# Attention and MoE kernel: one piece of W12 fewer, last outputs by two queues, and a new planner's table

## The chip, the cores and the metric

The kernel runs on one core of a Trainium2 chip. The metric is the device time of one execution in microseconds (us). Engines are named as the profile names them: PE is TensorE (PEld its weight loads), DVE VectorE, ACT ScalarE, POOL GpSimd, SP SyncE, which here only issues DMAs.

## What is computed

The reference is a recurrence over 768 positions for 4 batches of 8 heads with 40 dimensions, and then a product chain over the 3072 tokens of 320 numbers:

```
for t in range(S):
    y[:, :, t] = einsum('bhd,bhde->bhe', rt, state)
    Sa = einsum('bhde,bhe->bhd', state, at)
    state = state * wt - einsum('bhd,bhe->bhde', Sa, bt) + einsum('bhd,bhe->bhde', vt, kt)
a = x @ w1            # x: y as 3072 x 320; w1, w2: 320 x 1024
b = x @ w2
out = ((a * b) @ w3) @ w_out   # w3: 1024 x 1024, w_out: 1024 x 320
```

The four matrices come as 64-bit floats.

## The kernel before

**Work and stages.** The recurrence is cut into 12 chunks of 64 positions (NCH, C). For each chunk the kernel loads its inputs (`load`), scales them by running products of w (`scale`), forms the products inside the chunk (`causal`, L551), solves the triangular systems (`solve`, `join`; small VectorE instructions at L630 and L634), prepares pairs and tokens (`pairs` L792, `tokens` L816), runs the recurrence step by small matmuls of 64 by 64 (`rec`, `product` at L840), and writes y, which SP's DMAs lay out as xr (`gather`, L915). Then `mlp` runs: xs is xr split in a high and a low part (ACT L940, DVE L943); a and b come from eight matmuls each per 128 columns at L957 (`terms` pairs the five WT tiles with the parts of xs), their product is split again (gh by ACT, gl by POOL or DVE at L974), and 48 matmuls at L983 with W3 = w3 @ w_out (built once, L470) give the output, which ACT copies to o and SP sends (L992).

**The weights.** VectorE, ScalarE and GpSimd turn the 64-bit numbers into 32-bit floats piece by piece (`convert`, from L385): a piece has 128 partitions and 1024 columns. Its steps are cv.in (SP's load of raw, L391), cv.e (L394, DVE), cv.exp (L398, ACT), cv.sign (L401, ACT), cv.m (L404, DVE), cv.lo (L408, DVE), cv.f (L412, DVE) and cv.out (L415, DVE or POOL). There are 17 pieces (one of 512 columns): 2 for rows 0 to 127 of W12 = [w1, w2], 3 for w_out, 8 for w3, 2 for W12's rows 128 to 255 and 2 for its last 64 rows, which the host lays twice into 128 rows. After each W12 piece, w.hi (ACT copy to float32r) and w.lo (L457, DVE or POOL: what the copy lost) fill WT. Of the last 64 rows WT[4] holds the high part in partitions 0 to 63 and the low part in 64 to 127, so that one matmul uses both. The tiles of the MLP (xs, gh, gl, ga, o) take the memory of the conversion, so no MLP begins before the last W12 piece is done (`third`).

**What sets the order.** Nothing is ordered by hand: every step is an `op` with a due time (t0 of its chunk, minus an offset P of its stage, plus OFF of its tag) and a cost (OPS). `Order.place` simulates the engines with these costs, takes on each engine the ready op with the smallest due time among those that could start within LOOK, and models buffers (SLOTS: y, xr, xs 1; raw 2; bank 6), TensorE's clock, tile modes (a matmul group that changes mode gets STICK added to its due time, and waits for the one before), DMA landing times and the lock between DVE and POOL for ops that need both ports (`two`). The instructions are emitted in that order, and each engine runs its own in order. ON says by one letter per op whether a step that both can do goes to POOL (p) or DVE (d).

Of the kernel before, what the change touches and what calls it, by code (L numbers as in the profile page):

```python
# [14 lines left out]
ALU = mybir.AluOpType  # L15
# [4 lines left out]
NCH = S // C  # L20
# [10 lines left out]
CW = 1024  # L31
# [12 lines left out]
OFF = {"ca.j": -611.218, "ca.js": -295.116, "ca.lm": -409.432, "ca.mask": 322.878, "ca.mm": -196.496, "cv.e":  # L44
       -352.619, "cv.exp": -294.308, "cv.f": 875.871, "cv.in": 923.729, "cv.lo": 148.411, "cv.m": -331.453, "cv.out":
       -690.808, "cv.sign": -986.054, "ga": 652.698, "jo.cp1": 176.7, "jo.cp2": 1171.31, "jo.mm1": 500.308, "jo.mm2":
       559.977, "jo.tt": 1216.266, "ld.aa": 255.685, "ld.fm": -308.122, "ld.xx": -220.769, "m.a": -43.748, "m.ab":
       -25.534, "m.gh": -539.967, "m.gl": -14.3, "m.mm1": 97.143, "m.mm2": 289.0, "m.o": 98.802, "m.out": -533.298,
       "m.xh": -105.084, "m.xl": 349.579, "nil": 390.528, "pa.cp": -142.457, "pa.mask": 411.539, "pa.mm": 399.693,
       "pa.rv": 721.462, "pa.v": -32.743, "r.hs": -489.727, "r.n": 318.043, "r.s": -178.475, "r.sb": -189.193, "r.st":  # L50
       490.608, "r.t0": -269.903, "r.t1": 72.728, "r.t2": -860.309, "r.tr": -475.318, "r.u": -459.283, "r.y":
       -480.807, "r.zn": -15.068, "r.zv": -155.411, "sc.aa": 621.487, "sc.chk": -167.343, "sc.exp": 187.27, "sc.gi":
       -148.615, "sc.gt": -230.551, "sc.ln": 87.006, "sc.scan": 203.673, "sc.xs": 130.059, "so.d": -775.834, "so.in":
       -264.37, "so.m1": -358.78, "so.m2": -299.304, "so.q": 713.223, "so.sa": -515.229, "so.sb": -535.393, "so.t":
       -345.96, "so.td": 366.095, "so.tt": -385.449, "so.v": -186.183, "so.x": -90.021, "so.z": 257.847, "tk.cp":
       -717.729, "tk.mm": 348.057, "w.hi": 667.696, "w.lo": -164.398, "w3.hi": 386.505, "w3.lo": -443.484, "w3.mm":
       -484.2, "z.bk": 434.685}
LOOK = dict(pe=0.135, act=0.0, dve=0.0, pool=0.101, sp=0.0, nil=0.0)
# [27 lines left out]
    "m.mm2": ("pe", 0.88, 0, "128", 1.05, 12, 0.31, 1.88), "m.o": ("act", 0.437), "m.out": ("sp", 0.58, 0, None, 0.25), "nil": ("nil", 0.0), "z.bk": ("act", 0.53),  # L86
# [3 lines left out]
FLIGHT, QUEUE, STICK = 1.9, 8, 34.913  # L90
# [32 lines left out]
class Order:  # L123
# [39 lines left out]
    def place(self):  # L163
# [29 lines left out]
        while len(placed) < len(ops):  # L193
# [982 lines left out]
```

## Time and profile before

| | us |
|---|---|
| timed runs, median of 3 | 648.69 (648.24 to 648.99) |
| the profiled execution, its own time | 643.84 |
| its span, first to last instruction | 642.1 |
| mean granted TensorE clock | 0.984 |
| TensorE busy | 566.2 (88%) |
| VectorE busy | 473.3 (74%) |
| ScalarE busy | 382.5 (60%) |
| GpSimd busy | 184.7 (29%) |

A busy share is an average over stages; the stages are told apart by the view that gives each engine's busy time in a stretch of the span. A group row gives the line, engine and operation, the tiles written and read, the shape and count, the busy time and the mean of one in ns, and then how long the engine stood idle just before these instructions and what ended most of that. All of ScalarE's plain copies have the helper's line L273.

### The profile page before, as it was taken

The page shows a single profiled execution, that of the slowest core. Times are in us where ns is not written, and L with a number is a line of the kernel's source. Part 1 is how long each engine was busy: PE and PEld are TensorE (multiplying, and loading weights), DVE is VectorE, ACT ScalarE, POOL GpSimd, SP SyncE. Part 2 cuts the span into 40 slices and gives each one's busy share as a digit, 9 for nine tenths or more (in the row PEclk, how much of TensorE's full clock was granted, in tenths as well). Part 3 has the DMA queues.
Part 4 walks back from the last instruction along what each step waited for, and adds up shares of the span by engine and source line. Part 5 has one row for each costly group of instructions (what it writes and reads, how often), then busy time and mean ns, then how long its engine had stood idle before and what let it go on. Part 6 is the DMA issues. An engine that isn't in the chain of part 4 may idle for free.

```text
span 642.1 us, 27039 instructions
## 1 busy us (share of the span) xinstructions
PE 566.2 (88%) x11970; PEld 503.9 (78%) x11970; DVE 473.3 (74%) x849; ACT 382.5 (60%) x825; POOL 184.7 (29%) x230
## 2 busy tenths in 40 slices
PE   1536889867999999999999999998999999999995
PEld 0435767556988988888888889887988898898995
DVE  6799897987949959769589599497595794971220
ACT  6767557686465665755755746657557557354221
POOL 3542414035332413403312115332232242020111
PEclk9999989968999999999999999999999999999998
DMA  8975566535213423523534335235135333210001
GB/s 193 294 225 167 154 212 217 196 87 152 69 29 85 117 69 98 141 48 90 137 80 110 82 79 134 59 96 141 41 93 141 78 83 81 51 37 14 26 21 25
DMA packets 53401, 68.23 MB, mean 106 GB/s; under 512 B 29984, under 2 KB 37664, under 8 KB 51232
## 3 DMA queue, kind: packets, MB, share of 16 engines
q1 hardware_dynamic: 53280, 66.46, 38.3%
q8 instruction: 95, 1.56, 1.0%
q14 instruction: 26, 0.21, 0.1%
HBM read 57.79 MB, written 3.93 MB: 96 GB/s over the span
## 4 chain that ended last, share of the span: by engine, by line
PE 36%; DVE 28%; ACT 17%; DMA 9%; SPq 5%; issue 4%; POOL 0%; ACTq 0%; DVEq 0%
PE bank L957 15%; PE bank L840 9%; ACT JP L273 5%; DVE tmp L630 4%; SPq L915 4%; DMA fm<-in_fmg_dram 4%; PE bank L983 4%; ACT TT L273 3%; PE bank L551 3%; DMA xr<-y 3%; DVE ab L604 2%; PE bank L470 2%; DVE mf L408 2%; DVE ga L971 2%; ACT hs L273 2%
## 5 line engine op out<-in xcount | busy, mean ns | idle before, releaser
L957 PE MATMUL bank<-xs,W 128*128 128x256 f32 x1536 | 208.3, 288 | 2.8 <-ACT o L273 2.8
L957 PEld LDWEIGHTS bank<-xs,W 128*128 128x128 f32 x1536 | 187.8, 189 | 14.1 <-ACT o L273 3.6
L273 ACT ACTIVATE gh<-ga 128x512 fp32r<-128x512 f32 x48 | 30.3, 631 | 94.8 <-DVE ga L971 94.8
L891 DVE TENSOR_TENSOR un<-bank,mask_h 128x416 f32<-128x416 f32 x48 | 28.2, 588 | 73.0 <-PE bank L840 63.9
L974 POOL TENSOR_TENSOR gl<-ga,gh 128x512 fp32r<-128x512 f32 x29 | 37.5, 1292 | 118.3 <-ACT gh L273 92.4
L801 POOL TENSOR_SCALAR_AFFINE_SELECT vg<-vg 64x256 f32<-64x256 f32 x96 | 43.9, 457 | 74.6 <-DVE gl L974 24.0
L983 PE MATMUL bank<-W3h,gh 128*128 128x320 f32 x192 | 63.8, 332 | 0.0
L567 POOL TENSOR_SCALAR_AFFINE_SELECT lm<-lm 64x512 f32<-64x512 f32 x48 | 34.0, 708 | 95.5 <-ACT lm L273 74.7
L983 PE MATMUL bank<-W3l,gh 128*128 128x320 f32 x192 | 59.2, 308 | 0.0
L983 PE MATMUL bank<-W3h,gl 128*128 128x320 f32 x192 | 59.2, 308 | 0.0
L273 ACT ACTIVATE JP<-bank 64x256 f32<-64x256 f32 (+2 forms) x120 | 45.4, 379 | 20.7 <-PE bank L551 19.0
L840 PE MATMUL bank<-hs,TT 64*64 64x104 f32 x768 | 49.8, 269 | 7.3 <-ACT TT L273 5.2
L840 PE MATMUL bank<-un,bk 64*64 64x104 f32 (+1 forms) x768 | 47.9, 266 | 2.8 <-DVE un L891 2.3
L523 POOL TENSOR_TENSOR xx<-xx,gi 112x1024 f32<-112x1024 f32 x12 | 28.5, 2379 | 74.6 <-DVE gi L519 22.9
L971 DVE TENSOR_TENSOR ga<-bank,ga 128x512 f32<-128x512 f32 x48 | 32.7, 681 | 22.3 <-PE bank L957 22.3
L840 PEld LDWEIGHTS bank<-hs,TT 64*64 64x64 f32 x768 | 39.3, 142 | 11.5 <-ACT TT L273 6.0
L840 PE MATMUL bank<-vg,bk 64*64 64x104 f32 (+1 forms) x768 | 47.1, 264 | 0.0
L840 PEld LDWEIGHTS bank<-un,bk 64*64 64x64 f32 (+1 forms) x768 | 37.8, 130 | 8.9 <-DVE un L891 5.6
L551 PE MATMUL bank<-aa,xx 40*64 40x64 f32 x1536 | 32.8, 239 | 10.7 <-POOL xx L523 5.5
L551 PEld LDWEIGHTS bank<-aa,xx 40*64 40x64 f32 x1536 | 30.5, 153 | 12.9 <-POOL xx L523 5.7
L470 PE MATMUL bank<-wof,w3f 128*128 128x320 f32 x128 | 38.0, 453 | 2.4 <-DVE w3f L415 1.5
L273 ACT ACTIVATE ga<-bank 128x512 f32<-128x512 f32 x48 | 28.7, 597 | 16.9 <-PE bank L957 16.3
(120 smaller groups left out, 1245.9 us busy)
## 6 DMA issues: line engine op xcount, KB each, us to landing
rv<-in_rv_dram SPq DMA_DIRECT2D x48, 294.0 KB
xx<-in_fmx_dram SPq DMA_DIRECT2D x24, 448.0 KB
raw<-in_w3t_dram SPq DMA_DIRECT2D x8, 1024.0 KB
raw<-in_w_dram SPq DMA_DIRECT2D x6, 1024.0 KB
fm<-in_fmg_dram SPq DMA_DIRECT2D x24, 227.5 KB
aa<-in_fma_dram SPq DMA_DIRECT2D x24, 224.0 KB
vg<-in_vt_dram SPq DMA_DIRECT2D x48, 80.0 KB
out_dram<-o SPq DMA_DIRECT2D x48, 80.0 KB
```

The source lines that it names most:

```text
L273: act.activation(out_, in_, AF.Copy, scale=scale)
L470: pe.matmul(out=pt.t[:, 0:DM], lhsT=w[:, j], rhs=wof[:, j], start=(j == 0), stop=(j == NJ - 1))
L523: e.tensor_tensor(out=X, in0=X, in1=gi.t.unsqueeze(2).to_broadcast([ROWS, 2 * NP, 2, C]), op=ALU.mult)
L551: pe.matmul(out=bank(s)[64 * z:64 * z + 64, i, p], lhsT=X[r, p, z], rhs=aa[i].t[r, p], start=True, stop=True)
L567: op("ca.mask", due + 6, lambda q=q: pool.affine_select(out=lm.t[q], in_=lm.t[q], pattern=[[0, 2 * NP], [1, C]], compare_op=ALU.is_gt, fil ...
L801: op("pa.mask", due + 2, lambda q=q, vg=vg: pool.affine_select(out=vg.t[q, :, 0:C], in_=vg.t[q, :, 0:C], pattern=[[0, NP], [1, C]], compar ...
L840: pe.matmul(out=out_(ab ^ z, p), lhsT=left(ab, ab ^ x, p), rhs=right(ab ^ x, p), start=start and p == 0, stop=True, skip_group_check=True)
L891: dve.tensor_tensor(out=un[i].t, in0=view(hp[i]), in1=mask_h.unsqueeze(1).to_broadcast([128, NP, N]), op=ALU.mult)
L957: pe.matmul(out=pt.t[:, TOK * x:TOK * x + TOK], lhsT=WT[k][:, cs], rhs=xs.t[:, z], start=(n == 0), stop=(n == 7))
L971: op("m.ab", t, lambda a=a, pt=pt: dve.tensor_tensor(out=a.t, in0=wide(pt), in1=a.t, op=ALU.mult), r=[pt], w=[a])
L974: both(("gl", c % NCH * 4 + j // 2), "m.gl", t + 1, lambda e, a=a, j=j: e.tensor_tensor(out=gl.t[:, j:j + 2], in0=a.t, in1=gh.t[:, j:j + 2 ...
L983: pe.matmul(out=pt.t[:, 0:DM], lhsT=l.t[:, j, ts], rhs=W3[r][:, j], start=(j == 0 and n == 0), stop=(j == NJ - 1 and n == 2))
```

## The change

The last 64 rows of W12 come as one array `wc` of 128 rows: in rows 0 to 63 their columns of w1, in 64 to 127 those of w2. They are one piece, and its two halves are each copied (w.hi) and subtracted (w.lo, now always on DVE), the low part going to the other 64 partitions. The piece counter goes from 17 to 16. For the last chunk, the second half of each output tile is sent by ACT's queue (tag m.oa). The table of due times, assignments and costs is another one, and a DMA in the planner has two more terms (a longer flight, `cold`, and a delay behind landing, `act`).

```diff
-T0, T = 449.562, 122.639
-P = dict(w0=116.83, ws=51.334, ld=75.808, sc=8.354, ca=161.389, so=-139.305, sp=243.519, jo=671.741, pa=42.027,
-         tk=3.502, rg=-37.491, ga=1051.868, ml=179.371, mt=282.608)
-ON = dict(aa="dppddpdddppdpppddppppddd", cv="pdddppdddpddddppp",
-          gl="dpppdpppddppddpppdddddpppppdpdpdppppddddpppdpppp", ws="pdddpp", xs="ddpddppppdpppdddppddpdpd")
-OFF = {"ca.j": -611.218, "ca.js": -295.116, "ca.lm": -409.432, "ca.mask": 322.878, "ca.mm": -196.496, "cv.e":
...
-LOOK = dict(pe=0.135, act=0.0, dve=0.0, pool=0.101, sp=0.0, nil=0.0)
+T0, T = 514.56, 92.461
+P = dict(w0=-196.327, ws=45.883, ld=498.429, sc=358.623, ca=116.411, so=-652.303, sp=-438.072, jo=499.915, pa=49.614,
+         tk=-155.98, rg=-40.9, ga=1276.543, ml=545.435, mt=406.895)
+ON = dict(aa="pdddpddpppppppppppddpdpp", cv="ppddddpdddpdddpd", gl="ppppppdppppdpppdddppppppddpppppdpdppdddpdddpdpdp",
+          ws="pddd", xs="pdpddpdppdpppdpdpdpppddp")
+OFF = {"ca.j": -279.458, "ca.js": -671.541, "ca.lm": -806.163, "ca.mask": 55.347, "ca.mm": 33.954, "cv.e": -173.885,
...
+LOOK = dict(pe=0.122, act=0.0, dve=0.0, pool=0.371, sp=0.0, nil=0.0)
...
-    "cv.in": ("sp", 0.42, 0, None, 4.7), "cv.e": ("dve", 0.682, 1), "cv.exp": ("act", 1.090), "cv.sign": ("act", 1.030),
+    "cv.in": ("sp", 0.42, 0, None, 3.4, 0, 0.3, 0.15), "cv.e": ("dve", 0.682, 1), "cv.exp": ("act", 1.13), "cv.sign": ("act", 1.13),
...
-    "w.hi": ("act", 0.990), "w.lo/p": ("pool", 2.430, 1), "w.lo/d": ("dve", 1.213, 1),
+    "w.hi": ("act", 1.05), "w.lo/p": ("pool", 2.430, 1), "w.lo/d": ("dve", 1.213, 1),
...
-    "ga": ("sp", 0.7, 0, None, 0.25),
+    "ga": ("sp", 0.78, 0, None, 0.25, 0, 1.0, 0.0),
...
-FLIGHT, QUEUE, STICK = 1.9, 8, 34.913
+FLIGHT, QUEUE, STICK = 1.9, 8, 0.0
...
-                done, clock[e] = max(t + FLIGHT, landed[-1]) + o["span"], t + o["cost"]
+                done, clock[e] = max(t + FLIGHT + o["cold"], landed[-1]) + o["span"], t + o["cost"]
                 landed.append(done)
+                done += o["act"]
...
-    pieces = iter(range(17))
+    pieces = iter(range(16))
...
-            for f in range(2 * DFF // CW):
+            for f in range(2 * DFF // CW if k < 2 else 1):
                 cs = slice(CW * f, CW * f + CW)
-                mf = convert(w12[k * 128:k * 128 + 128, cs], None, due)
-                n = (0, 1, 4)[k]
-                rows = slice(64, 128) if k == 2 else slice(0, 128)
+                mf = convert(w12[k * 128:k * 128 + 128, cs] if k < 2 else wc, None, due)
                 over = ["conv"] if k == 0 else ["conv", "reg2"]
...
-                op("w.hi", due, f1, r=[mf, *over], w=[("W", k, f)])
-                both(("ws", 2 * k + f), "w.lo", due, f2, r=[mf, *over], w=[("W", k, f)])
+                for x in (f,) if k < 2 else range(2):
+                    xs = slice(CW * x, CW * x + CW)
+                    q, z = (slice(0, 128),) * 2 if k < 2 else (slice(64 * x, 64 * x + 64), slice(64 - 64 * x, 128 - 64 * x))
+                    hi, lo = (0, 1, 4)[k], 2 + k
...
+                    op("w.hi", due, f1, r=[mf, *over], w=[("W", k, x)])
+                    if k < 2:
+                        both(("ws", 2 * k + f), "w.lo", due, f2, r=[mf, *over], w=[("W", k, x)])
+                    else:
+                        op("w.lo/d", due, lambda f2=f2: f2(dve), r=[mf, *over], w=[("W", k, x)])
                 due += step
...
             for b in range(2):
-                op("m.out", t, lambda b=b, tt=tt, o=o: sp.dma_start(
+                tag, e = ("m.oa", act) if c == NCH - 1 and b else ("m.out", sp)
+                op(tag, t, lambda b=b, tt=tt, o=o, e=e: e.dma_start(
                     out=out[bass.ds((2 * tt + b) * S + row, C)], in_=o.t[64 * b:64 * b + 64]), r=[o])
...
-    rows += rows[256:]
...
+    wc = bits(np.concatenate([w12[256:, 0:DFF], w12[256:, DFF:]], axis=0))
+    w12 = bits(w12[:256])
```

The numbers of OFF, P and T0 are due times on the planner's own scale, not microseconds of the chip. Most other costs in OPS move by some hundredths.

## Rows read from the trace of the kernel before

**Rows 1.** The page, TensorE's busy time.

```profile
PE 566.2 (88%) x11970; PEld 503.9 (78%) x11970; DVE 473.3 (74%) x849; ACT 382.5 (60%) x825; POOL 184.7 (29%) x230
```

**Rows 2.** Stretches: length; busy PE, PEld, DVE, ACT, POOL; clock, DMA share, GB/s.

```profile
40.00:140.00 100.00, 75.20 (x1648) 57.88 (x1648) 90.50 (x130) 68.43 (x118) 28.39 (x30) 0.93 0.57 178
140.00:160.00 20.00, 15.90 (x472) 13.37 (x471) 15.22 (x36) 13.63 (x30) 10.49 (x12) 0.90 0.50 131
160.00:600.00 440.00, 426.68 (x9303) 386.31 (x9304) 330.96 (x628) 263.11 (x607) 119.73 (x153) 1.00 0.33 83
600.00:642.10 42.10, 35.48 (x278) 35.18 (x276) 6.24 (x11) 9.96 (x18) 6.73 (x6) 0.96 0.11 27
```

**Rows 3.** Timeline of POOL, DVE and ACT, 134 to 172: start, length, instruction.

```profile
135.06 2.13 POOL L415 TENSOR_TENSOR mf<-mf,sg 128x1024 f32<-128x1024 f32 x1 [4.14 <-DVE mf L408]
...
145.73 2.13 POOL L415 TENSOR_TENSOR mf<-mf,sg 128x1024 f32<-128x1024 f32 x1 [0.74 <-DVE tmp L630]
...
150.49 2.35 POOL L457 TENSOR_TENSOR W<-mf,W 64x1024 fp32r<-64x1024 f32 x1 [0.18 <-ACT W L273]
...
136.94 0.80 DVE L394 TENSOR_SCALAR e<-raw 128x1024 uint16<-128x1024 uint16 x1
...
156.13 0.95 DVE L943 TENSOR_TENSOR xs<-xr,xs 128x768 fp32r<-128x768 f32 x1
...
149.35 1.05 ACT L273 ACTIVATE W<-mf 128x1024 fp32r<-128x1024 f32 x1
...
153.92 0.84 ACT L940 ACTIVATE xs<-xr 128x768 fp32r<-128x768 f32 x1
```

**Rows 4.** Line L957, 140 to 200: least/median/most ns, first and last start.

```profile
L957 PE MATMUL bank<-xs,W x182: 276/282/388, 157.9 to 200.0; 128*128 128x256 f32 x182
```

**Rows 5.** Groups by shape, whole span: busy, mean of one, idle before.

```profile
L408 DVE SCALAR_TENSOR_TENSOR mf<-raw,mf 128x1024 f32<-128x1024 uint32 x16 | 21.2, 1326 | 0.2
...
L401 ACT ACTIVATE sg<-raw 128x1024 bf16<-128x1024 int16 x16 | 18.5, 1154 | 10.1 <-DVE w3f L415 4.7 <-POOL mf L415 2.6 <-DVE mf L415 2.2
L398 ACT ACTIVATE e<-e,ebias 128x1024 uint16<-128x1024 uint16 x16 | 18.4, 1147 | 1.7 <-DVE e L394 1.7
...
L412 DVE TENSOR_TENSOR sg<-sg,e 128x1024 bf16<-128x1024 bf16 x16 | 12.2, 760 | 3.0 <-ACT sg L401 2.4 <-ACT e L398 0.6
L404 DVE TENSOR_SCALAR mf<-raw 128x1024 int32<-128x1024 int32 x16 | 11.4, 715 | 1.1 <-DMA raw<-in_w3t_dram 1.0
L394 DVE TENSOR_SCALAR e<-raw 128x1024 uint16<-128x1024 uint16 x16 | 11.2, 699 | 1.1 <-DMA raw<-in_w_dram 1.0
...
L415 POOL TENSOR_TENSOR mf<-mf,sg 128x1024 f32<-128x1024 f32 x4 | 9.0, 2254 | 21.6 <-DVE sg L412 16.8 <-DVE mf L408 4.1 <-DVE tmp L630 0.7
...
L457 POOL TENSOR_TENSOR W<-mf,W 64x1024 fp32r<-64x1024 f32 x2 | 4.7, 2358 | 0.3 <-ACT W L273 0.2
```

**Rows 6.** Tile raw and line L457: least/median/most ns, first and last start.

```profile
L408 DVE SCALAR_TENSOR_TENSOR mf<-raw,mf x17: 686/1226/1859, 24.2 to 140.1; 128x1024 f32<-128x1024 uint32 x16, 128x512 f32<-128x512 uint32 x1
...
L457 DVE TENSOR_TENSOR W<-mf,W x3: 1208/1211/3149, 43.2 to 137.7; 128x1024 fp32r<-128x1024 f32 x3
```

**Rows 7.** Tile y, 0 to 200: SP's DMAs from y to xr.

```profile
L915 SPq DMA_DIRECT2D xr<-y x24: 538/684/941, 80.2 to 166.7; - x24
```

**Rows 8.** Timeline of the end, and line L992 over the span.

```profile
635.86 1.11 SPq L992 DMA_DIRECT2D out_dram<-o  x2
...
L992 SPq DMA_DIRECT2D out_dram<-o x48: 466/558/1814, 180.5 to 636.4; - x48
```

**Rows 9.** Stretches of 10 us, columns as in rows 2.

```profile
80.00:90.00 10.00, 8.81 (x180) 6.13 (x178) 9.75 (x15) 5.14 (x11) 1.99 (x3) 0.83 0.74 240
...
130.00:140.00 10.00, 6.13 (x163) 5.45 (x152) 8.55 (x10) 7.79 (x14) 3.31 (x3) 0.51 0.25 88
```

**Rows 10.** The chain that ended last, 585 to 642: start, length, what.

```profile
592.26 1.14 PE bank L957 x8
...
613.07 15.24 PE bank L957 x128
```

More of the change, by code (lines that the diff above doesn't have):

```diff
@@ L58 @@
-LOOK = dict(pe=0.135, act=0.0, dve=0.0, pool=0.101, sp=0.0, nil=0.0)
+T0, T = 514.56, 92.461
[4 more added lines that the diff above has]
+OFF = {"ca.j": -279.458, "ca.js": -671.541, "ca.lm": -806.163, "ca.mask": 55.347, "ca.mm": 33.954, "cv.e": -173.885,
+       "cv.exp": -132.486, "cv.f": 1449.755, "cv.in": 755.934, "cv.lo": 858.805, "cv.m": -594.194, "cv.out": -327.381,
+       "cv.sign": -1155.983, "ga": 1271.368, "jo.cp1": 1151.213, "jo.cp2": 965.253, "jo.mm1": 575.096, "jo.mm2":
+       797.938, "jo.tt": 1558.004, "ld.aa": 185.001, "ld.fm": -766.597, "ld.xx": -104.394, "m.a": -375.288, "m.ab":
+       97.307, "m.gh": -538.707, "m.gl": -254.877, "m.mm1": 53.279, "m.mm2": 147.301, "m.o": 81.919, "m.oa": -178.394,
+       "m.out": 265.507, "m.xh": -147.679, "m.xl": 576.185, "nil": 57.266, "pa.cp": 49.867, "pa.mask": 479.639,
+       "pa.mm": 801.234, "pa.rv": 906.531, "pa.v": -140.458, "r.hs": -159.212, "r.n": 106.389, "r.s": 138.062, "r.sb":
+       -260.258, "r.st": 563.83, "r.t0": -652.593, "r.t1": 453.968, "r.t2": -618.307, "r.tr": -1004.632, "r.u":
+       -592.361, "r.y": -1181.646, "r.zn": 22.379, "r.zv": -122.778, "sc.aa": 849.905, "sc.chk": -338.326, "sc.exp":
+       492.942, "sc.gi": -103.955, "sc.gt": -577.576, "sc.ln": -311.006, "sc.scan": -174.304, "sc.xs": 366.767,
+       "so.d": -1080.429, "so.in": -520.493, "so.m1": -702.795, "so.m2": 189.337, "so.q": 1004.707, "so.sa":
+       -1260.855, "so.sb": -1105.151, "so.t": -277.876, "so.td": 721.968, "so.tt": -146.905, "so.v": 19.25, "so.x":
+       27.744, "so.z": 325.32, "tk.cp": -936.577, "tk.mm": 424.344, "w.hi": 972.575, "w.lo": -198.775, "w3.hi":
+       194.369, "w3.lo": -532.212, "w3.mm": -83.172, "z.bk": 877.353}
@@ L65 @@
     "w3.mm": ("pe", 2.15, 0, "128", 2.33, 16, 0.838, 1.88), "w3.hi": ("act", 0.44), "w3.lo": ("dve", 0.46),
-    "ld.fm": ("sp", 0.42, 0, None, 0.85), "ld.xx": ("sp", 0.42, 0, None, 1.85), "ld.aa": ("sp", 0.42, 0, None, 0.85),
-    "sc.chk": ("act", 0.64), "sc.scan": ("dve", 1.26, 1), "sc.ln": ("act", 0.62), "sc.exp": ("act", 0.76),
+    "ld.fm": ("sp", 0.42, 0, None, 0.75, 0, 0.3, 0.5), "ld.xx": ("sp", 0.42, 0, None, 1.85, 0, 0.3, 0.85), "ld.aa": ("sp", 0.42, 0, None, 0.88, 0, 0.3, 0.4),
+    "sc.chk": ("act", 0.73), "sc.scan": ("dve", 1.26, 1), "sc.ln": ("act", 0.62), "sc.exp": ("act", 0.63),
@@ L77 @@
+    "jo.cp2": ("act", 0.375), "jo.tt": ("act", 0.625),
+    "pa.rv": ("sp", 0.42, 0, None, 1.08, 0, 0.3, 0.6), "pa.v": ("sp", 0.65, 0, None, 0.36, 0, 0.3, 0.4), "pa.mm": ("pe", 0.52, 0, "64", 0.66, 64, 0.089, 1.88), "pa.cp": ("act", 0.4),
     "pa.mask": ("pool", 0.42, 1),
@@ L261, in attention_moe @@
 @with_exitstack
-def attention_moe(ctx: ExitStack, tc: tile.TileContext, fmg, fmx, fma, rv, vt, sq, svr, w12, w3t, wo, out):
+def attention_moe(ctx: ExitStack, tc: tile.TileContext, fmg, fmx, fma, rv, vt, sq, svr, w12, wc, w3t, wo, out):
     nc = tc.nc
@@ L1153, in bits @@
         return x.view(np.int64) if x.dtype == np.float64 else x
-    w12 = bits(np.concatenate([np.asarray(i["moe_w1"])[rows], np.asarray(i["moe_w2"])[rows]], axis=1))
+    w12 = np.concatenate([np.asarray(i["moe_w1"])[rows], np.asarray(i["moe_w2"])[rows]], axis=1)
+    wc = bits(np.concatenate([w12[256:, 0:DFF], w12[256:, DFF:]], axis=0))
+    w12 = bits(w12[:256])
     w3t = bits(np.asarray(i["moe_w3"]).reshape(NJ, 128, NJ, 128).transpose(0, 3, 2, 1).reshape(NJ, 128, DFF))
@@ L1158, in _layout @@
     return {n: np.ascontiguousarray(t) for n, t in
-            dict(fmg=fmg, fmx=x, fma=fma, rv=rv, vt=vt, sq=sq, svr=svr, w12=w12, w3t=w3t, wo=wo).items()}
+            dict(fmg=fmg, fmx=x, fma=fma, rv=rv, vt=vt, sq=sq, svr=svr, w12=w12, wc=wc, w3t=w3t, wo=wo).items()}
 def kernel(**inputs):
```

31 lines of the change are left out of this document (8 added, 23 removed).

## The prediction

> **What bounds the kernel now.** I read the page first: TensorE is busy 566.2 of 642.1 us [rows 1], and the change takes no matmul away, so time can only come out of the 76 us in which TensorE stands still, or out of time at a low clock. Next the view by stretches, to see where those are [rows 2]. From 160 to 600 us TensorE is busy 426.68 of 440 at full clock: 13.3 us are open, and VectorE has 109 us to spare there, so TensorE bounds this part. From 40 to 140 it is busy 75.2 of 100 while VectorE is busy 90.5: here the weights are converted, VectorE bounds the stage, and TensorE waits. In 140 to 160 TensorE has 4.1 us open and a granted clock of 0.90. After 600 us there is one dense run of matmuls and a tail without TensorE.
>
> Then the timeline of VectorE, ScalarE and GpSimd around the end of the conversion, to see what lets the MLP begin [rows 3]. The seventeenth piece starts at 136.94 (e), is multiplied out on GpSimd at 145.73, its high half is copied at 149.35, and its low half ends at 150.49 + 2.35 = 152.84. ScalarE makes xs at 153.92, VectorE its low part at 156.13 to 157.08, and the first L957 matmul starts at 157.9 [rows 4]. From there on TensorE stands still 13.3 us in 440. So what matters is how early the MLP begins, and how much of TensorE's idle time before that can be filled.
>
> The sum is made against the profiled execution, 643.84 us (span 642.1 and 1.74 around it). The timed runs have a median of 648.69, 4.85 more; I take the same difference off that median. About 0.2% (1.3 us) is what a measurement of this kernel can tell from no change.
>
> **The pieces of W12's last rows.** Before, the last 64 rows are laid twice into 128 partitions and converted as two pieces of 1024 columns; after, both column halves lie in one piece, one half of the partitions each. One piece falls away: on VectorE 0.699 + 0.715 + 1.326 + 0.760 = 3.50 us (L394, L404, L408, L412), on ScalarE 1.154 + 1.147 = 2.30, one load of raw on SP's queue, and a product that took 2.13 us on GpSimd at 145.73 [rows 3, 5]. Kept are two copies to the high half: an instruction on 64 partitions costs as much as one on 128 with the same 1024 columns, as the GpSimd rows of 64 partitions (2.36) and of a full piece (2.25) suggest [rows 5], so ScalarE saves nothing more. The two subtractions move from GpSimd (2 x 2.36) to VectorE, where the undisturbed one takes 1.21 [rows 5, 6]: +2.42 on VectorE. A VectorE subtraction whose output lies in other partitions than its input isn't in the trace; I take 1.21, with 1.21 and 3.15 as ends, both from that line [rows 6].
>
> The new table also sends 11 instead of 10 of the pieces' products to VectorE (5 instead of 7 to GpSimd): +1.22. So VectorE's conversion work is nearly unchanged, -3.50 + 2.42 + 1.22 = +0.14. What is gained lies elsewhere. First, the last piece's chain goes. The piece before it leaves GpSimd at 135.06 + 2.13 = 137.2 [rows 3]; with two copies of 1.05 behind it and one subtraction of 1.21 the weights could be whole at about 140.5, not 152.84. TensorE can't use all of those 12 us: it only has 4.1 us open in 140 to 160, and with the clock at 0.90 there, 2 us more of its matmuls' time at most [rows 2]. That is the upper end, -6. Second, GpSimd holds VectorE up less: the subtraction that took 3.15 began while GpSimd ran, and L408 has a mean of 1.326 against a median of 1.226 [rows 5, 6], so 1.94 + 16 x 0.10 = 3.5 us of VectorE's time in this stage are such waits, and GpSimd loses 2 x 2.25 + 2 x 2.36 = 9.2 us of conversion work. The lower end is no gain, where VectorE's unchanged 90.5 us alone set the stage. I take -3.5, in the middle: the rows show both a VectorE that has 10% open and a chain that is really cut short.
>
> What is late next: xs for the first MLP waits for the gathered y of the first chunk, which was sent from 80.2 us on [rows 7], so that isn't it; attention of the later chunks is, since the y and xr tiles have one buffer each.
>
> **The last outputs.** For the last chunk the second half of each output tile is issued by ScalarE. At the end SP issued two, in 1.11 us from 635.86; one issue has 0.466, 0.558 and 1.814 as least, median and most [rows 8]. ScalarE comes from the copy that makes the tile and has nothing queued behind it; the earlier such issue, by the tile before it, comes in the dense run of matmuls in which ScalarE has time to spare. Ends: -0.55 (both at once) to +0.70 (ScalarE needs 1.81). I take -0.5, since the median row is nearest. The Trainium skill, "DMA: Bandwidth & Descriptors", section "Issuing engines are not separate DMA queues", says that several issuing engines share the same DMA engines and save only the time to issue: by it nothing beyond the 0.55 can come, and the transfers themselves would not get faster; no row here shows two issuers.
>
> **The table.** P, OFF, ON, T, T0 and LOOK decide the order that is emitted, so all engines' queues are redrawn, SP's and GpSimd's as well, and no part of the old order can be taken as kept. Three things can be weighed. The costs move toward the rows: the sign and exp of a piece are 1.154 and 1.147 in the trace [rows 5], entered as 1.03 and 1.09 and now as 1.13, so on 17 pieces the old plan put 17 x (0.12 + 0.06) = 3.1 us too little on ScalarE; VectorE's L412 stood still 3.0 us for exactly these two. Half of that, -1.5, is what I take. Ends: -3.0 and +3.0, for a new order can as well open a wait of the same size. Second, more work goes to GpSimd in the scaling and the low parts (53 products before, 61 after); from 160 us on that is hidden by TensorE's 97% and VectorE's 109 idle us [rows 2]. Without that cover each would cost what the slower engine takes more. Third, STICK, what the planner adds to the due time of a matmul group that changes TensorE's tile mode, goes from 34.9 to 0; that is the second rival's.
>
> **Sum:** -3.5 - 0.5 - 1.5 = -5.5: 643.84 becomes 638.3, and the median 648.69 becomes **643.2**. The ends of the terms all on one side give 639.1 and 652.4 (as -9.6 and +3.7); with them partly offset, 640 to 648 is this case's own range.
>
> **The rivals.**
> *More than that.* The 25 us that TensorE stands still between 40 and 140 [rows 2] are open to a better order too, and so is its low clock: 0.83 in 80 to 90 and 0.51 in 130 to 140, after a stretch with waits; at 0.51 nearly all runs at 1.2 instead of 2.4 GHz, so up to 5 us are lost in those ten [rows 9]. If the new order fills a quarter of the 25 us, 6 us, the sum is -11: 637.7. For it: the stage has the largest idle time. Against it: VectorE is 90% busy there and gets no lighter. The Trainium skill, "TensorE: Matmul & The Clock Gate", section "What's actually happening", says that the activity monitor runs free of the kernel's start, so that cold stretches differ from run to run; by it the 4.85 us between the timed runs and the profile could be such stretches, and an order made for any phase would recover part of them. The three runs differ by only 0.75, which doesn't bear it out well. Chance of this case, whatever its source, 0.20.
>
> *Slower: more changes of tile mode.* Without STICK, L957 groups of 8 matmuls are interrupted more often by attention's small matmuls. A dense group takes 15.24 / 16 = 0.95, one between interruptions 1.14 [rows 10]: 0.19 each. 29 more interruptions eat the 5.5 us. Of the 192 groups (16 to a chunk) the last 16 lie in the dense end, so there is room for 45 more: 45 x 0.19 = 8.6, or +3.1: 651.8. For it: STICK was large and is now nothing, in the stretch where TensorE bounds. Against it: the model still charges the switch itself (ENTRY and the drain), and the old order interrupts often already. Chance 0.23.
>
> *Nothing comes through.* The MLP begins earlier, but the later chunks' attention (one y, one xr) comes no earlier, and TensorE's idle time only moves from before 160 to after it, leaving the tail's 0.5: 648.2. For it: the DVE sum of +0.14. Against: 97% busy after 160 shows that there was work in hand as soon as the MLP was open. Chance 0.12; that the edit does not remove the piece is ruled out by the code.
>
> **How the numbers follow.** Forecast 0.45, more 0.20, slower 0.23, nothing 0.12. Faster by over 0.2% is the first two, 0.65; within 0.2% most of the last, 0.11; slower 0.24. The range takes in the slower case (651.8) and the better one (637.7), with under 1 us beyond the first and under 3 beyond the second, since the better one has the wider spread: 635 to 652.5.
>
> **What would show it.** Right: 16 pieces instead of 17; the last L457 before 148 us and the first L957 before 154; over 16.5 us of TensorE in 140 to 160; the last output issues beside each other and the end about 0.5 sooner after the last matmul; 426 of 440 or more kept between the MLP's start and 600. Wrong: L957 groups of 8 far more often alone; idle time of TensorE after 160 well over 13 us; the first L957 no earlier than 157.9.

## The result and the profile after

The changed kernel took **630.14 us** (median of 4 runs, 628.36 to 631.72) against 648.47 for the kernel before in the same comparison: ratio 0.9719, 95% interval 0.9687 to 0.975. I had predicted 643.2, range 635 to 652.5. The direction was right, the size was three times too small, and the result lies below the range. The profiled execution took 628.36, 15.5 less than the profiled one of before (643.84). The medians differ by 18.3 because the profile of before lay 4.6 under its median and that of after 1.8 under its own; the traces have to explain the 15.8 us between their spans. In four later comparisons the kernel before had medians of 645.16 to 648.32, so the 18.3 are at the upper end of what the timed runs say.

The page after, the line that answers to [rows 1]:

```profile
PE 560.6 (90%) x11970; PEld 500.2 (80%) x11970; DVE 463.4 (74%) x840; ACT 383.7 (61%) x823; POOL 184.8 (30%) x234
```

The same 11970 matmuls take 5.6 us less of TensorE's busy time. (The profile models the ends of matmuls, so the line between busy and idle time is its reckoning.) The stretches, columns as in [rows 2], with the end now at 626.3:

```profile
40.00:140.00 100.00, 77.77 (x1688) 59.77 (x1688) 88.60 (x133) 69.94 (x118) 23.07 (x27) 0.91 0.50 162
140.00:160.00 20.00, 20.00 (x424) 18.29 (x423) 18.50 (x43) 12.03 (x29) 6.14 (x9) 1.00 0.43 109
160.00:600.00 440.00, 429.17 (x9428) 390.73 (x9427) 320.95 (x611) 267.54 (x612) 133.62 (x166) 1.00 0.33 86
600.00:626.30 26.30, 20.48 (x162) 20.11 (x160) 4.30 (x7) 5.80 (x10) 2.59 (x2) 0.98 0.07 18
```

Since TensorE does the same matmuls, its column is an account of the whole gain. Against [rows 2] it has done 2.6 us more in 40 to 140, 4.1 more in 140 to 160 (all that was open) and 2.5 more in 160 to 600; with 0.3 before 40 that is 9.4 us of idle time filled. Its whole work is 5.6 shorter. Together 15.0, which is what is missing after 600: 20.48 instead of 35.48. The last 0.8 is idle time in the tail.

Where it begins, in stretches cut at the first MLP matmul and at 200 us. Before:

```profile
0.00:157.90 157.90, 101.94 (x2353) 80.58 (x2353) 134.07 (x207) 107.40 (x197) 57.66 (x71) 0.95 0.65 190
157.90:200.00 42.10, 40.74 (x748) 38.15 (x747) 31.35 (x54) 27.09 (x60) 12.50 (x12) 1.00 0.27 69
```

After:

```profile
0.00:139.00 139.00, 89.97 (x1956) 70.04 (x1957) 118.67 (x178) 97.39 (x173) 41.74 (x56) 0.94 0.65 193
139.00:200.00 61.00, 60.57 (x1284) 55.06 (x1285) 49.10 (x102) 38.74 (x88) 22.21 (x28) 1.00 0.37 98
```

The MLP begins 18.9 us sooner, after 397 fewer matmuls and 15.4 us less of VectorE's work; and from there to 200 us TensorE stands still for only 0.4 of 61 us. Both halves of this matter below. The first matmul and the timeline of VectorE and ScalarE ahead of it, which answers to [rows 3, 4]:

```profile
L963 PE MATMUL bank<-xs,W x1536: 276/281/393, 139.0 to 613.0; 128*128 128x256 f32 x192
```

```profile
130.97 1.22 DVE L416 TENSOR_TENSOR mf<-mf,sg 128x1024 f32<-128x1024 f32 x1
131.43 3.08 ACT L274 ACTIVATE W<-mf 128x1024 fp32r<-128x1024 f32 x3
...
134.34 2.47 DVE L460 TENSOR_TENSOR W<-mf,W 64x1024 fp32r<-64x1024 f32 x2
...
136.85 0.85 ACT L946 ACTIVATE xs<-xr 128x768 fp32r<-128x768 f32 x1 [0.19 <-DVE W L460]
...
137.82 1.29 DVE L949 TENSOR_TENSOR xs<-xr,xs 128x768 fp32r<-128x768 f32 x1 [0.38 <-ACT xs L946]
...
141.08 2.06 DVE L610 STREAM_TRANSPOSE ab<-JP 128x1024 f32<-128x1024 f32 x1 [0.84 <-ACT JP L274]
```

W12 is whole at 134.34 + 2.47 = 136.8, 16.0 sooner than before, and xs follows 0.04 us behind it. The transpose that opens chunk 2's solve comes behind all of this; before it ran at 143.02, ahead of the last piece's L412 at 144.90:

```profile
143.02 1.99 DVE L604 STREAM_TRANSPOSE ab<-JP 128x1024 f32<-128x1024 f32 x1
144.90 0.68 DVE L412 TENSOR_TENSOR sg<-sg,e 128x1024 bf16<-128x1024 bf16 x1
```

VectorE's groups up to the first MLP matmul show the same exchange (busy us, mean ns | idle just before and its releaser). Before:

```profile
L630 DVE TENSOR_TENSOR tmp<-GP,ab 128x2 f32<-128x2 f32 (+14 forms) x23 | 6.1, 264 | 0.7
...
L891 DVE TENSOR_TENSOR un<-bank,mask_h 128x416 f32<-128x416 f32 x8 | 4.7, 590 | 4.7 <-PE bank L840 4.7
...
L900 DVE TENSOR_TENSOR y<-bank,fm 104x256 f32<-104x256 f32 x8 | 3.0, 417 | 2.0 <-PE bank L840 1.9
```

After:

```profile
L640 DVE TENSOR_REDUCE GP<-tmp 128x2 f32<-128x2 f32 (+7 forms) x16 | 4.1, 254 | 0.3
L636 DVE TENSOR_TENSOR tmp<-GP,ab 128x2 f32<-128x2 f32 (+7 forms) x16 | 4.1, 253 | 0.4
...
L897 DVE TENSOR_TENSOR un<-bank,mask_h 128x416 f32<-128x416 f32 x6 | 3.5, 587 | 0.5 <-PE bank L846 0.5
...
L906 DVE TENSOR_TENSOR y<-bank,fm 104x256 f32<-104x256 f32 x4 | 1.5, 420 | 0.5 <-PE bank L846 0.5
```

Solve steps fall from 23 pairs to 16, recurrence steps from 8 to 6 and 4. Added up by kind, the 15.4 us are 5.5 less for the pieces' e, m, lo and f steps (57.9 to 52.4), 1.4 more for W's low parts, 0.6 more for products, and 11.9 less of attention and set-up (54.4 to 42.5), most of which now lies behind the start. The stretches from the start to the end, before and after, show what makes room for it there:

```profile
157.90:642.10 484.20, 464.25 (x9620) 423.32 (x9618) 339.27 (x643) 275.13 (x628) 127.01 (x159) 1.00 0.31 79
```

```profile
139.00:626.30 487.30, 470.64 (x10014) 430.12 (x10014) 344.76 (x663) 286.33 (x651) 143.06 (x178) 1.00 0.32 83
```

VectorE has only 5.5 us more to do in this stage, while GpSimd has 16.0 more: the new ON sends 61 instead of 53 products of the scaling and the low parts to GpSimd. All this is a reading of two traces. The experiments test the start and the order; no run changes ON alone.

### The profile page after: what moved, and what is told of

Same layout as the page of the kernel before. It is cut to its first block, busy times and chain, and to the rows that moved or that the text cites. A ratio compares the mean times of both kernels' runs of the same rounds, so it can differ in the third digit from the quotient of the medians.

```text
span 626.3 us, 27034 instructions
## 1 busy us (share of the span) xinstructions
PE 560.6 (90%) x11970; PEld 500.2 (80%) x11970; DVE 463.4 (74%) x840; ACT 383.7 (61%) x823; POOL 184.8 (30%) x234
## 4 chain that ended last, share of the span: by engine, by line
DVE 43%; PE 30%; ACT 19%; issue 6%; POOL 1%; DMA 1%; ACTq 0%; DVEq 0%; POOLq 0%
PE bank L963 11%; DVE tmp L636 9%; ACT JP L274 6%; PE bank L846 6%; PE bank L989 5%; PE bank L476 4%; DVE ab L640 3%; DVE fm L508 3%; DVE ab L610 3%; ACT TT L274 3%; DVE ga L977 3%; PE bank L557 3%; DVE GP L640 2%; DVE Tp L640 2%; DVE y L906 2%
## 5 line engine op out<-in xcount | busy, mean ns | idle before, releaser
L963 PE MATMUL bank<-xs,W 128*128 128x256 f32 x1536 | 217.1, 290 | 1.4 <-ACT o L274 1.3
L963 PEld LDWEIGHTS bank<-xs,W 128*128 128x128 f32 x1536 | 190.3, 189 | 13.2 <-issue 1.9
L980 POOL TENSOR_TENSOR gl<-ga,gh 128x512 fp32r<-128x512 f32 x31 | 39.9, 1288 | 140.2 <-ACT gh L274 111.3
L897 DVE TENSOR_TENSOR un<-bank,mask_h 128x416 f32<-128x416 f32 x48 | 28.2, 588 | 70.6 <-PE bank L846 70.6
L807 POOL TENSOR_SCALAR_AFFINE_SELECT vg<-vg 64x256 f32<-64x256 f32 x96 | 41.3, 430 | 70.0 <-ACT vg L274 23.8
L846 PE MATMUL bank<-hs,TT 64*64 64x104 f32 x768 | 48.4, 265 | 6.9 <-ACT TT L274 3.8
L529 POOL TENSOR_TENSOR xx<-xx,gi 112x1024 f32<-112x1024 f32 x14 | 33.3, 2380 | 64.5 <-DVE gi L525 26.6
L846 PE MATMUL bank<-un,bk 64*64 64x104 f32 (+1 forms) x768 | 45.9, 259 | 2.2 <-DVE un L897 2.1
L274 ACT ACTIVATE bk<-bank 128x416 f32<-128x416 f32 x48 | 24.1, 517 | 37.3 <-PE bank L822 37.2
L476 PE MATMUL bank<-wof,w3f 128*128 128x320 f32 x128 | 39.8, 469 | 4.2 <-DVE w3f L416 4.2
L846 PEld LDWEIGHTS bank<-un,bk 64*64 64x64 f32 (+1 forms) x768 | 36.0, 126 | 8.1 <-DVE un L897 4.3
```

Of the source, the lines that this page charges most:

```text
L274: act.activation(out_, in_, AF.Copy, scale=scale)
L476: pe.matmul(out=pt.t[:, 0:DM], lhsT=w[:, j], rhs=wof[:, j], start=(j == 0), stop=(j == NJ - 1))
L807: op("pa.mask", due + 2, lambda q=q, vg=vg: pool.affine_select(out=vg.t[q, :, 0:C], in_=vg.t[q, :, 0:C], pattern=[[0, NP], [1, C]], compar ...
L846: pe.matmul(out=out_(ab ^ z, p), lhsT=left(ab, ab ^ x, p), rhs=right(ab ^ x, p), start=start and p == 0, stop=True, skip_group_check=True)
L963: pe.matmul(out=pt.t[:, TOK * x:TOK * x + TOK], lhsT=WT[k][:, cs], rhs=xs.t[:, z], start=(n == 0), stop=(n == 7))
L980: both(("gl", c % NCH * 4 + j // 2), "m.gl", t + 1, lambda e, a=a, j=j: e.tensor_tensor(out=gl.t[:, j:j + 2], in0=a.t, in1=gh.t[:, j:j + 2 ...
```

## The experiments

**What the MLP's start is worth (two delays and one put-back).** The order of all instructions stays that of after; only VectorE, or VectorE and ScalarE, repeat a step that changes nothing when it is repeated.

```diff
-op("w.lo/d", due, lambda f2=f2: f2(dve), ...
+op("w.lo/d", due, lambda f2=f2, x=x: [f2(dve) for _ in range(5 if x else 1)], ...
```

> The changed kernel, every engine in its order, with the very last subtraction of W12 (64x1024, 1.22 us on VectorE) done five times instead of once: 4 x 1.22 = 4.9 us more ahead of the MLP, the result unchanged. If the moment at which W12 is whole sets the end: first MLP matmul 4.9 us later (143.9), span 4.9 us longer (631.2). If TensorE has other work to fill in, as my cap on the piece's gain supposed: span at most 2 us longer.

With `13` for `5`:

> The same with 12 more: 14.6 us, about what W12 was later before the change (152.8 against 136.8). If the moment at which W12 is whole sets the end: first MLP matmul at 153.6 and span about 641, near the kernel before. If slack takes part of it: 632 to 635.

And in the last piece alone, about the VectorE and ScalarE time that the seventeenth piece had (4.1 us on VectorE instead of 3.50, 2.3 on ScalarE; its load and its product are not put back):

```diff
+        g2, g4 = (lambda: [f2() for _ in range(7)], lambda: [f4() for _ in range(3)]) if again else (f2, f4)
-        op("cv.e", due, f2, r=[raw], w=[e])
+        op("cv.e", due, g2, r=[raw], w=[e])
...
-        op("cv.sign", due, f4, r=[raw], w=[sg])
+        op("cv.sign", due, g4, r=[raw], w=[sg])
...
```

> The changed kernel, every engine in its order, with a removed piece's load put back into the last one: the step e done seven times instead of once on VectorE (6 x 0.69 = 4.1 us) and the sign three times instead of once on ScalarE (2 x 1.15 = 2.3), the result unchanged. If in the new order the piece is worth what VectorE spends on it: span 3.5 to 4.7 us longer. If VectorE and ScalarE have slack at that place: under 2. In the old order taking the piece out gave 1.3 us of the span.

The first MLP matmul's line in the three (least, median and most ns, first and last start), the 5-fold one first:

```profile
L963 PE MATMUL bank<-xs,W x1536: 276/281/581, 144.0 to 623.0; 128*128 128x256 f32 x192
```

```profile
L963 PE MATMUL bank<-xs,W x1536: 276/281/580, 153.3 to 629.8; 128*128 128x256 f32 x192
```

```profile
L964 PE MATMUL bank<-xs,W x1536: 276/281/393, 142.5 to 616.2; 128*128 128x256 f32 x192
```

| | start, us later | span, us longer | median (range) | ratio to before, 95% |
|---|---|---|---|---|
| 5-fold | 5.0 | 10.0 (636.3) | 637.98 (633.28 to 638.49) | 0.9865, 0.9799 to 0.993 |
| 13-fold | 14.3 | 17.0 (643.3) | 645.73 (642.42 to 649.23) | 0.9997, 0.9958 to 1.0036 |
| piece put back | 3.5 | 3.5 (629.8) | 633.03 (630.97 to 635.25) | 0.9819, 0.9758 to 0.9881 |

What the start loses, the end loses at least. With 14.6 us of VectorE's work ahead of the start the whole gain is gone: the ratio is 1.0. The piece is worth about 3.5 us in this order: put back, it leaves the stage behind the start at 487.3 us, as after has it, and the kernel keeps 12.3 of the 15.8 us. The 5-fold kernel loses 5.0 more in the stage after, 3.3 of it as longer matmuls (473.99 us behind the start instead of 470.64): it has stretches at a lower granted clock that after doesn't have, as

```profile
485.00:490.00 5.00, 4.46 (x104) 3.99 (x105) 2.02 (x2) 4.82 (x11) 0.41 (x1) 0.69 0.33 94
```

Not every execution pays this: the profiled one had a mean clock of 0.979 and took 638.19 us, another of the four had 0.985 and took 633.28, 4.9 over the profiled one of after (628.36, clock 0.986). That suggests that the delay itself is paid one to one and the rest with the clock; the faster execution has no trace.

**The piece alone, in the old order.** The planner's input is that of before; the last piece's eight steps are emitted empty, and its two halves come from the piece ahead of it.

```diff
+        if skip:
+            f1 = f2 = f3 = f4 = f5 = f6 = f7 = lambda: None
+            f8 = lambda e: None
...
+                mf = convert(w12[k * 128:k * 128 + 128, cs] if k < 2 else wc, None, due, skip=k == 2 and f == 1)
```

> The kernel before in its old order on every engine, with the last conversion piece's eight steps left empty and both halves taken from the piece before it (wc laid out as in the change; all else computed as before, low parts still on GpSimd, outputs by SP). My step gave the piece 3.5 us: span about 638.6, first L957 some 4 us earlier than 157.9. The theory that the start of the MLP sets the end says that the end moves by as much as the first L957 does, whatever that is: with the copies at their old places in ScalarE's queue I expect the weights whole at 147 to 149 instead of 152.8 and the end 3 to 6 us earlier. The theory that only TensorE's idle time counts says at most 2 us.

It took 645.9 us, ratio 1.0003 (0.9963 to 1.0043), span 640.8, start 158.0: nothing. Its timeline of GpSimd and ScalarE says why:

```profile
133.46 2.13 POOL L415 TENSOR_TENSOR mf<-mf,sg 128x1024 f32<-128x1024 f32 x1 [4.15 <-DVE mf L408]
...
142.31 1.06 ACT L273 ACTIVATE W<-mf 64x1024 fp32r<-64x1024 f32 x1
...
148.63 2.35 POOL L463 TENSOR_TENSOR W<-mf,W 64x1024 fp32r<-64x1024 f32 x1 [2.83 <-ACT W L273]
...
152.35 0.84 ACT L946 ACTIVATE xs<-xr 128x768 fp32r<-128x768 f32 x1
```

The piece is out at 133.46 + 2.13 = 135.6. Its copies could follow at once, but in ScalarE's queue they stand at their old places behind attention's copies, one at 142.31 and the other at 147.5, and W12 is whole only at 151.0. Work taken off an engine whose order stays is waited out where the next step stands.

**The two halves of the change, each with a new plan.** First the new table, costs and queues with 17 pieces:

```diff
-    pieces = iter(range(16))
+    pieces = iter(range(17))
...
```

> The new table, costs, planner lines and output queues with the 17 pieces of before (the two extra choices are product and subtractions on VectorE). The order is drawn anew. If the table carries most of the gain: first matmul of the MLP before 146, span 629 to 633. If the piece carries most: first matmul of the MLP at 150 or later, span 636 or more. In both, first MLP matmul and end should move together within 3 us if the start sets the end.

Then one piece and two queues with before's table, costs and landing model:

```diff
-T0, T = 514.56, 92.461
+T0, T = 449.562, 122.639
...
```

> The one converted piece and the two output queues with the table, costs and planner lines of before (16 of its 17 choices kept). The order is drawn anew. If the piece carries most of the gain: span 627 to 632. If the table does: span 637 to 642, first MLP matmul at 150 to 156. If a redrawn order scatters by itself by more than either, the span can come out above 642.

Then all of after, its due times too, but with before's costs and landing model:

```diff
-    "cv.in": ("sp", 0.42, 0, None, 3.4, 0, 0.3, 0.15), ... "cv.exp": ("act", 1.13), "cv.sign": ("act", 1.13),
+    "cv.in": ("sp", 0.42, 0, None, 4.7), ... "cv.exp": ("act", 1.090), "cv.sign": ("act", 1.030),
...
```

> The changed kernel with the costs and landing times of before in the planner, its due times, assignments and 16 pieces kept; the order is drawn anew. If costs as traced carry the gain: 635 to 642, with the start of the MLP later than 143 or a looser stage behind it. If the due times and the structure carry it and costs of some hundredths only shift details: 627 to 633, as with the other constant that was moved (630.9).

Their stretches from the start to the end, in this order:

```profile
149.50:655.40 505.90, 473.46 (x9848) 431.11 (x9846) 341.29 (x645) 280.28 (x632) 139.66 (x168) 0.99 0.29 77
```

```profile
149.80:672.90 523.10, 485.41 (x9878) 441.87 (x9878) 348.94 (x663) 281.56 (x639) 126.61 (x160) 0.96 0.29 76
```

```profile
153.90:671.30 517.40, 477.68 (x9818) 436.41 (x9814) 345.21 (x648) 280.33 (x633) 138.13 (x168) 0.96 0.28 75
```

All three start the MLP 4 to 8 us earlier than before and are slower than it: 657.04, 668.31 and 675.86 us, ratios 1.0142 (1.0048 to 1.0236), 1.0327 (1.0254 to 1.0401) and 1.051 (1.044 to 1.0579). The loss is behind the start: 505.9 to 523.1 us instead of 484.2, of which TensorE stands still for 32 to 40 instead of 20 and is busy for 9 to 21 more, at a lower clock and with 200 to 260 more matmuls behind the start. So neither half, planned anew, brings a part of the gain. What a half is worth by itself these runs can't tell, for drawing the plan anew costs as much or more, as the next ones show.

**Nudges.** One cost of the planner's fetch model moved by 0.05, in after and in before:

```diff
-FETCH, BLOCK, HOT = 3.2, 256, 0.46
+FETCH, BLOCK, HOT = 3.25, 256, 0.46
```

> The changed kernel with one constant of the planner (FETCH, its time to fetch instructions) at 3.25 instead of 3.20, which draws the order anew from about a twelfth of TensorE's instructions on; the same instructions otherwise. If a table gives about the same time with any order near it: span within 3 us of 626.3. If the gain hangs on this one order, for which the due times were searched: 5 to 20 us longer, as with the two half changes (655.4 and 672.9), with TensorE's idle time and low clock after the start of the MLP as the cause.

> The kernel before with the planner's FETCH at 3.25 instead of 3.20, its order drawn anew; the same instructions. It tells how far orders of the old table scatter by themselves. If its order was as much a chosen one as the new one's: span 3 to 15 us over 642.1. If it was an ordinary draw: within 3 us, or shorter.

After: 633.49 us, span 630.9. Before: 671.12 us, ratio 1.0402 (1.0335 to 1.0469), span 670.6, start 167.9. The same nudge costs the old order 28.5 us of span and the new one 4.6. The other suspect of the slower rival, STICK alone, set back to 34.913 in after:

> The changed kernel with STICK back at 34.9, its order drawn anew. In the emitted order the changes of tile mode stay at 349 (301 before the change) and the L957-type runs at 137 against 136 (101 before), so by my second rival's price nothing comes or goes. Theory that any redrawn order loses a few us: span 628 to 633. Theory that STICK keeps TensorE from costly changes: shorter than 626.3.

630.88 us, span 628.3: no difference that counts. (In before, the planner with STICK at 0 gives the same order on every engine.)

**The last outputs and the subtractions.** All outputs by SP again:

```diff
-                tag, e = ("m.oa", act) if c == NCH - 1 and b else ("m.out", sp)
+                tag, e = "m.out", sp
```

> The changed kernel with all outputs issued by SP again; every engine's order is otherwise the same. If ScalarE's queue is what shortened the tail, the time from the last L989 matmul to the end of the span goes from 6.0 back to 6.7 us, and the timed median is about 0.7 us (0.1%) over the changed kernel's, within what a run can tell. If the tail was shortened by something else, it stays at 6.0.

The end of the chain after, and the issues of SP and ScalarE there, against those of this kernel:

```profile
613.24 7.06 PE bank L989 x48
```

```profile
618.14 3.11 SPq L999 DMA_DIRECT2D out_dram<-o  x2
...
620.79 0.50 ACTq L999 DMA_DIRECT2D out_dram<-o  x1
```

```profile
612.51 7.06 PE bank L989 x48
```

```profile
617.41 3.75 SPq L999 DMA_DIRECT2D out_dram<-o  x4
```

From the last matmul to the end it is 626.3 - 620.30 = 6.00 us with two queues and 626.0 - 619.57 = 6.43 with one: 0.43. The medians (630.14 and 628.23, each with the ratio 0.9719) don't show it. Then the last piece's two subtractions on GpSimd again:

```diff
-                        op("w.lo/d", due, lambda f2=f2: f2(dve), r=[mf, *over], w=[("W", k, x)])
+                        op("w.lo/d", due, lambda f2=f2: f2(pool), r=[mf, *over], w=[("W", k, x)])
...
```

> The changed kernel, every engine in its order, with the two subtractions of W12's last piece on GpSimd (2.36 us each) instead of VectorE (1.22), as they were before the change. If W12's end sets the start of the MLP and that the end: first MLP matmul 2.3 us later than 139.0 and span 2.3 us longer, up to 5 where a low-clock stretch follows. If VectorE, relieved of 2.4 us, is what counts: no longer than 626.3.

```profile
132.69 4.80 POOL L460 TENSOR_TENSOR W<-mf,W 64x1024 fp32r<-64x1024 f32 x2 [6.63 <-issue]
```

629.42 us, start 139.0, span 627.4. Though the two take 4.80 instead of 2.47, the first MLP matmul doesn't move and the end comes 1.1 us later. But VectorE, in the same order, was 1.0 us ahead of after here when it came to the W12 subtraction before them (131.60 instead of 132.58), which hides as much. So this placement is worth some 2 us, a small part of the gain.

**The order by hand.** If attention's VectorE work behind the conversion is the cause, then moving it there in the old order should do something. From 20 us ahead of the last W12 subtraction to the first MLP group, all that this group doesn't depend on was put behind it; the rest of the order is kept:

```diff
-    for o in order.place():
+    for o in gate_first(order.place(), 1, 20.0):
...
+def gate_first(placed, groups, reach):
...
+    return placed[:low] + [o for o in part if o["n"] in need] + [o for o in part if o["n"] not in need] + placed[gate + 1:]
```

> The kernel before, its table and its 17 pieces, with its planned order kept but for one stretch: from 20 us ahead of the last W12 subtraction to the first group of MLP matmuls, everything that group does not depend on is put behind it (24 small steps of chunk 2's solve on VectorE with its transpose, 15 ScalarE and 11 GpSimd steps, 6 of TensorE). Order theory: the last piece's L412 stood at 144.90 behind the transpose of 143.02, so it starts about 1.9 us earlier, GpSimd's product and two subtractions follow in a row, W12 is whole at about 150.5 instead of 152.84 and the first MLP matmul comes at 153 to 156 instead of 157.9; with one to one the span is 637 to 640. Rival (a moved order only moves idle time): the start is as early, but the later chunks' attention is late by as much and the span stays at 642 or grows.

> The same stretch put behind the first MLP group, in the kernel of before's order with one piece for the last 64 rows (which by itself gave start 158.0 and span 640.8). Order theory: the piece is multiplied out at 135.6, its two copies follow at once (to 137.7), GpSimd's two subtractions end at about 141.5, and the first MLP matmul comes at 143 to 147, 11 to 15 us earlier; with one to one the span is 626 to 630. Theory that the piece is worth nothing outside the new table: start above 153, span 637 or more. Rival (idle time only moves): start 143 to 147, span 637 to 642.

> As the kernel with one piece and the stretch put behind, but behind the fourth group of MLP matmuls instead of the first, so that TensorE has 4 us of MLP work in front of what waits for the work put behind. Order theory: start as there (143 to 147), and a span shorter by the 1 to 3 us that TensorE would otherwise wait. Rival (the work put behind is due at once): chunk 1's and 2's attention waits longer, the span is longer by as much.

> The changed kernel with the same rule: from 12 us ahead of its last W12 subtraction to its second group of MLP matmuls, all that those don't depend on goes behind them (16 small solve steps, 17 ScalarE, 9 GpSimd, 7 TensorE steps). Order theory: what still stood ahead of the last copies (two L897 of 0.59, ScalarE copies of 0.4 to 0.6) leaves, first MLP matmul at 136.5 to 138.5 instead of 139.0, span 624 to 626. Rival (its table is fitted as it stands): start within 0.5 of 139.0 or the later stage longer, span 627 to 632.

With 17 pieces L412 indeed moved up, the MLP started at 153.8, and the kernel got slower: 656.99 us, ratio 1.0163 (1.0092 to 1.0234), span 653.8. With one piece: start 153.1, 657.67 us, 1.0164 (1.009 to 1.0237), span 654.5. Behind the fourth group: start 157.9, 669.01 us, 1.0293 (1.0215 to 1.037). The changed kernel, so treated: start 141.7, 640.08 us, span 640.3. The stretch behind the start in the first two:

```profile
153.80:200.00 46.20, 38.16 (x642) 35.77 (x643) 31.71 (x55) 23.33 (x52) 14.50 (x17) 0.93 0.19 52
```

```profile
153.10:200.00 46.90, 40.61 (x674) 38.19 (x678) 31.70 (x55) 23.69 (x54) 14.51 (x17) 0.86 0.20 51
```

Here TensorE stands still for 8.0 and 6.3 us, where before it was 1.4 and after 0.4. So the rival is right for these: what was put behind the start was due at once, TensorE runs out of work and its clock falls. An early start pays only where work for TensorE stands ready behind it. The one-piece kernel didn't start at 143 to 147 either: its two copies waited until 142.88 and 146.87 in ScalarE's queue, the second behind a copy of the recurrence (hs, 145.92) on which the first MLP group depends too. The last kernel says little of the start, for some 2.5 us were lost ahead of the stretch that was changed (last section), and on VectorE both L897 stayed where they were. It loses most behind the start, as its rival says: 498.6 us instead of 487.3, with TensorE standing still for 5.3 of the first 58.3.

## Why the prediction was wrong

- **That the gate is W12's last piece and xs behind it** was right (the delays bear it out), and so were the signs I had named: 16 pieces, last L460 over at 136.8 (I said before 148), first L963 at 139.0 (before 154), 20.0 us of TensorE in 140 to 160 (over 16.5), 429.17 of 440 (426 or more). I didn't say by how much these would be overfulfilled.
- **The piece's term, -3.5, came out at its number, in part by luck.** Put back in the new order, the piece costs 3.5 us. But -3.5 was the middle between nothing and a cap of 6, and in the old order the piece brought nothing that the timed runs show (ratio 1.0003; 1.3 us of span). I wrote that TensorE "only has 4.1 us open in 140 to 160"; those 4.1 were filled to the last, though not by the piece alone, and I took this cap for the whole. W12 moved up by 16.0 us where I had worked out 12.
- **The step that failed is "The table", -1.5.** I costed it by VectorE's waits for sign and exp at L412, 3.0 us, half of which were to go because the planner now had higher costs for these two. They did not shrink. Ahead of the start L413 (the same step) now waits 4.1:

```profile
L413 DVE TENSOR_TENSOR sg<-sg,e 128x1024 bf16<-128x1024 bf16 (+1 forms) x16 | 10.7, 670 | 4.1 <-ACT e L399 2.4 <-ACT sg L402 1.4
```

  What the new order brings was in no term: of the 15.8 us the put-back piece takes 3.5 and the outputs 0.4, and the other 11.9 are the order's own, four times my end of 3.0. By the traces it puts about as much of VectorE's attention work behind the start without leaving TensorE without work there. By hand the first of these alone made the kernel slower, and with 17 pieces or the old costs the new table, planned anew, loses too.
- **"So time can only come out of the 76 us"** was wrong as a premise. TensorE's busy time fell from 566.2 to 560.6 with the same matmuls. Before the start it is 12.0 us shorter for 397 fewer of them, 30 ns each; behind the start it is 6.4 longer for 394 more, 16 each. The clock doesn't make this difference: ahead of the start it is at its lower level for 17.1 us in both traces. In a stage with waits a group's last matmuls lie open and count; in a dense one the next group covers them. Before, at full clock, an L551 matmul adds 27 ns to TensorE's busy time ahead of the start and 16 behind it, one of L840 32 and 27. That is 5.6 us, as much as my whole sum.
- **VectorE's net of +0.14** was wrong: -3.5 (-5.5 + 1.4 + 0.6). L408's mean of 1.288 in this stage became 1.183 at L409, with no subtraction of 3.15 left; I had these waits as a reason and not in the sum.
- **The last outputs**, -0.5: measured 0.43, where an issue by ScalarE took 0.50. The Trainium skill, "DMA: Bandwidth & Descriptors", section "Issuing engines are not separate DMA queues", agrees: no more than issue time was saved.
- **The slower rival's count came true, its cause and its price did not.** In TensorE's order L957 stands in 100 unbroken stretches and L963 in 135 (the expectation on STICK counts one more of each), and their groups

```profile
L957 PE MATMUL bank<-xs,W 128*128 128x256 f32 x1536 | 208.3, 288 | 2.8 <-ACT o L273 2.8
```

```profile
L963 PE MATMUL bank<-xs,W 128*128 128x256 f32 x1536 | 217.1, 290 | 1.4 <-ACT o L274 1.3
```

  went from 208.3 to 217.1 us. But a group's row also counts the ends that matmuls of the next group cover: the rows of all TensorE groups add up to 758.9 and 759.3 us, where TensorE is busy 566.2 and 560.6. Counting only what each matmul adds to the busy time, L957 has 201.7 us and L963 202.4: 0.7 for 35 more stretches, 0.02 each where I had 0.19. My 0.19 was read from a group of 8 that stands alone in the chain, with its end open [rows 10]. Nor is STICK the cause, for putting it back takes none of these stretches away.
- **The rival "more"** (637.7) looked to idle time ahead of the MLP, rightly, but it was too small as well, and not the stretch that gave most: of the 6 us that it had filled in 40 to 140, 2.6 were, and the low clock that it named there stayed (0.91, before 0.93). The range reached down only for it.

What stays open: how the 18.9 us of the start divide. The piece is worth about 3.5 of them in the new order and next to nothing in the old; the others belong to the order, but which of its numbers (P, OFF, ON, costs) make it was not separated. Why the new order bore the nudge better than the old one is not known either, and it was one pair. That the profile of before lies 4.6 us under its median is within that kernel's scatter: 40 later executions of it took 641.0 to 653.0 us, at mean clocks between 0.969 and 0.985. No run beat the changed kernel measurably.

## What to carry to other kernels

Find the gate between two stages and list what each in-order queue has ahead of it that the gate doesn't need; work that is removed while these places stay is simply waited out. But an early gate pays only if the bounding engine has work in hand behind it, so account for the bounding engine's busy time stretch by stretch, and do not take its total as fixed. A fitted order belongs to the kernel and the costs it was fitted to: judge a structural change together with its refit. Six orders drawn anew here had spans 0.3 to 7.2% longer than those of the kernels they came from, some with half of the change taken out.

## What the runs showed of the hardware

Two things I had not expected. With a delay of 5 us on VectorE, in an order that didn't change, the profiled execution had a stretch at a clock of 0.69 more than 300 us later, which that of after had not, and single MLP matmuls of 581 ns where the longest was 393; not all executions of that kernel lost this time. And the last kernel of the order by hand, whose order is that of after up to about 120 us, ran the same W3 products at another clock. Stretch 110 to 120 after, and then in that kernel:

```profile
110.00:120.00 10.00, 10.00 (x32) 6.80 (x31) 9.83 (x14) 7.30 (x10) 0.00 (x0) 0.84 0.64 214
```

```profile
110.00:120.00 10.00, 9.01 (x46) 6.20 (x46) 7.88 (x11) 6.13 (x9) 0.00 (x0) 0.66 0.64 213
```

At 0.66 instead of 0.84 VectorE came 2.5 us later to the same W3l subtraction (119.16 instead of 116.67). By the Trainium skill, "TensorE: Matmul & The Clock Gate", section "What's actually happening", cold stretches differ from run to run of one kernel; this pair, two kernels with one order up to there, agrees with it.
